# The seventh product's sum in the routing's PSUM banks, and a new order of steps, in the 512-token pages

## The chip, the cores and the metric

The kernel runs on one core of one Trainium2 chip. The metric is the device time of one execution in microseconds, the median of the runs shown. Matrix products run on TensorE (PE in the profile; its weight loads are PEld), elementwise work on VectorE (DVE) and ScalarE (ACT), indirect DMAs are issued by GpSimd (POOL) and all other DMAs by SyncE (SP). Each engine works through its own instructions in the order in which the kernel wrote them, and waits for the other engines where data or a buffer asks for it. TensorE writes its sums to PSUM, which has eight banks; one bank holds 128 x 512 float32 values.

## The reference

A gated scan over four sequences of 5056 tokens with 256 channels gives y, and y goes through a mixture of eight experts, of which each token uses one:

```python
a_t = np.exp(8.0 * sig_r * np.log(a_base))
x_gated = np.sqrt(np.maximum(1.0 - a_t * a_t, 1e-06)) * sig_i * x
for t in range(S):
    h = a_t[:, t] * h + x_gated[:, t]
    y[:, t] = h

logits = x @ w_gate + modality_bias[modality_id]
e_idx = np.argmax(logits, axis=1)
gate_w = probs[np.arange(N), e_idx]
for e in range(E):
    mask = e_idx == e
    h = np.maximum(x[mask] @ w1[e], 0.0)
    out[mask] = gate_w[mask, None] * (h @ w2[e])
```

There are N = 20224 tokens, D = 256 channels and FF = 1024 hidden units.

## The kernel before

**Stages.** The sequences are loaded in 23 chunks; each is scanned, split into two float16 parts (a high part and the rest), and routed: TensorE computes the logits, VectorE the places, and the tokens' rows are written to DRAM sorted by expert. Two experts get most tokens, and their weights stay on the chip. From the sorted rows the kernel builds pages of one expert's tokens: a few of 128, most of 256, and, once all chunks are loaded and sums of weight blocks are there, pages of 512 (`WIDE`). Experts with few tokens get 128-token pages with weights of their own, which ScalarE and VectorE convert (`cw`).

**The order.** A planner in the kernel writes every engine's instructions in order while the kernel is built. Each piece of work is a thread that names its engine, a length and a condition (`room` of a buffer tag, or a mark that something is `seen`); the planner takes what can start first. Times in it only decide the order; on the chip, waits are set by the data and the buffers.

**A page on TensorE.** `expert_layers` (from L1335) runs the first layer of a page in steps, and after each step some units of the second layer of the page before. A unit is three matmuls with 256 columns (two float16 parts of each operand, without the product of the two rests); a step of a 512-token page is six of them. `share` (L1285) says how many 32nds of the units follow each step; a 512-token page has 32 units, eight to each 128 tokens, a 256-token page has 16, a 128-token page 8.

**The 512-token pages.** Their first layer treats X·W1 as 2 x 2 blocks in Strassen's manner (Winograd's form): seven products instead of eight. `go(g, i)` issues product i for group g (half of the hidden units of each half), so a page has 14 steps, (0,1) to (1,4). A group has three PSUM sums of one bank each:

- `pa` (bank 1): product 1, then 2 on top. ScalarE copies product 1 into pb before that (`seed`, L1227).
- `pb` (bank 2): starts from that copy; 6, 5 and 3 are added. After 6 and after 5, ScalarE copies the sum out (v and v5, L1199).
- `pc` (bank 5): product 7; VectorE adds v5 (c22, L1204); then 4 on top, and VectorE adds v (c21).

Each of the four results goes through `relu_pair`: a relu on ScalarE (L1103) gives the high part, VectorE (L1105) the rest, into `Hx` and `Hg`, which the second layer reads. v, v5, c21 and c22 of a group lie in one buffer `sv` of tag `a` (three buffers, which the token sums `rf` also use). The sums of tokens T, which products 4 to 7 take, are made on VectorE and ScalarE from X while the page before runs.

**PSUM.** Tag `ph` has four banks, `po` (second layer) two, and `lg` two, which the routing uses (`psl`). In the 512-token pages pa, pb and pc all take banks of `ph` in turn, six to a page. A bank comes free when its last reader is done. A page's first use of a bank for pb needs a matmul before it that wrote the whole bank; where the bank last held a 128-token page, a matmul without use (L1247) writes it.

## Time and profile before

| | us |
|---|---|
| median of 3 runs | 978.96 |
| lowest, highest | 977.93, 980.19 |
| the profiled execution | 988.55 |
| its span, first to last instruction | 986.7 |
| TensorE busy in it | 878.6 |
| VectorE, ScalarE, GpSimd busy | 698.9, 671.0, 481.5 |

The profiled execution is one run with the hardware profiler; its durations and waits are those of that run. A row of a wait names who waited, for whom, the total, how often, and the longest. A row of the timeline gives a start, a duration, the engine, the line of the kernel, what was written from what, and in brackets how long the engine had been idle and what ended that. Matmul ends are modelled, so that groups of matmuls overlap a little on paper. A granted clock of 1.00 is TensorE's full speed.

### The profile page before, as it was taken

The page shows a single profiled execution, that of the slowest core. Times are in us where ns is not written, and L with a number is a line of the kernel's source. Part 1 is how long each engine was busy: PE and PEld are TensorE (multiplying, and loading weights), DVE is VectorE, ACT ScalarE, POOL GpSimd, SP SyncE. Part 2 cuts the span into 40 slices and gives each one's busy share as a digit, 9 for nine tenths or more (in the row PEclk, how much of TensorE's full clock was granted, in tenths as well). Part 3 has the DMA queues.
Part 4 walks back from the last instruction along what each step waited for, and adds up shares of the span by engine and source line. Part 5 has one row for each costly group of instructions (what it writes and reads, how often), then busy time and mean ns, then how long its engine had stood idle before and what let it go on. Part 6 is the DMA issues. An engine that isn't in the chain of part 4 may idle for free.

```text
span 986.7 us, 22224 instructions
## 1 busy us (share of the span) xinstructions
PE 878.6 (89%) x8461; PEld 775.3 (79%) x8461; DVE 698.9 (71%) x1535; ACT 671.0 (68%) x960; POOL 481.5 (49%) x506
## 2 busy tenths in 40 slices
PE   2358995989999998999999999998899999999896
PEld 1247884878888887888888888877788888888786
DVE  5976886697886787799678789686675656645451
ACT  6876886776887787897767989544655545444542
POOL 5233464577766676667575667363451111112121
PEclk9988997999999999999999999999999999999998
DMA  8757885878989798996889976965332222112410
GB/s 294 213 151 182 257 245 110 230 192 179 288 224 229 168 248 230 214 207 196 187 225 236 260 194 167 155 137 147 96 92 55 60 49 49 45 45 64 125 35 23
DMA packets 222759, 160.43 MB, mean 163 GB/s; under 512 B 197297, under 2 KB 201522, under 8 KB 216114
## 3 DMA queue, kind: packets, MB, share of 16 engines
q1 hardware_dynamic: 205714, 114.49, 51.0%
q0 software_dynamic: 16224, 44.25, 13.9%
q8 instruction: 68, 1.11, 0.5%
q14 instruction: 49, 0.40, 0.1%
q10 hardware_dynamic: 704, 0.18, 0.1%
HBM read 72.96 MB, written 44.48 MB: 119 GB/s over the span
## 4 chain that ended last, share of the span: by engine, by line
PE 53%; DVE 14%; issue 9%; DMA 9%; ACT 8%; POOL 3%; SPq 1%; another core or an unknown queue 0%; POOLq 0%; ACTq 0%; DVEq 0%
PE po L1326 26%; PE ph L1166 17%; PE pb L1256 4%; PE pc L1256 3%; DVE x L546 3%; DMA rows<-rt,di 3%; PE pa L1256 2%; DVE H L1105 2%; DMA rt<-a 2%; DMA X<-rows 2%; POOL out_dram L1121 2%; POOL rows L813 2%; DVE g L517 1%; ACT H L1103 1%; DVE x L531 1%
## 5 line engine op out<-in xcount | busy, mean ns | idle before, releaser
L1166 PE MATMUL ph<-X,hw 128*128 128x256 f16 (+1 forms) x2688 | 334.3, 276 | 23.7 <-DMA X<-rows 21.7
L1121 POOL DMA_INDIRECT out_dram<-ot,mt x160 | 206.6, 1291 | 282.5 <-ACT ot L1117 239.5
L1326 PE MATMUL po<-hw,H 128*128 128x256 f16 x2640 | 330.1, 274 | 11.4 <-issue 7.5
L1166 PEld LDWEIGHTS <-hw 128*128 128x128 f16 x2688 | 261.6, 100 | 57.9 <-DMA X<-rows 15.4
L813 POOL DMA_INDIRECT rows<-rt,di x158 | 214.9, 1360 | 183.6 <-PE ph L1166 44.7
L1326 PEld LDWEIGHTS <-H 128*128 128x128 f16 x2688 | 259.1, 98 | 46.9 <-issue 12.9
L1105 DVE SCALAR_TENSOR_TENSOR H<-ph,H 128x512 f16<-128x512 f32 (+1 forms) x232 | 151.6, 664 | 79.9 <-ACT H L1103 62.6
L1103 ACT ACTIVATE H<-ph 128x512 f16<-128x512 f32 (+1 forms) x232 | 132.9, 577 | 106.4 <-PE ph L1166 70.6
L1117 ACT ACTIVATE ot<-po,gt 128x256 f32<-128x256 f32 x160 | 75.3, 472 | 87.7 <-PE po L1326 75.8
L546 DVE TENSOR_TENSOR_SCAN x<-a,x 128x2048 f32<-128x2048 f32 (+2 forms) x23 | 87.9, 3821 | 0.8
L1326 PE MATMUL po<-hw,Hg 128*128 128x256 f16 x576 | 83.5, 273 | 0.0
L1326 PE MATMUL po<-hw,Hx 128*128 128x256 f16 x576 | 80.2, 273 | 0.6 <-ACT ot L1117 0.6
L1256 PEld LDWEIGHTS <-sw 128*128 128x128 f16 x576 | 56.5, 98 | 28.2 <-issue 21.5
L1326 PEld LDWEIGHTS <-Hx 128*128 128x128 f16 x576 | 56.2, 98 | 7.2 <-issue 0.7
L1326 PEld LDWEIGHTS <-Hg 128*128 128x128 f16 x576 | 56.4, 98 | 6.5
L663 ACT ACTIVATE a<-x,scy 128x1024 f16<-128x1024 f32 (+2 forms) x46 | 45.8, 1021 | 17.5 <-DVE scy L289 15.3
L531 DVE TENSOR_TENSOR x<-g,x 128x2048 f32<-128x2048 f32 (+2 forms) x23 | 45.8, 1989 | 16.4 <-ACT x L529 14.4
L1204 DVE TENSOR_TENSOR sv<-pc,sv 128x512 f32<-128x512 f32 x48 | 33.1, 690 | 29.6 <-PE pc L1256 16.2
L1199 ACT ACTIVATE sv<-pb 128x512 f32<-128x512 f32 x48 | 28.6, 595 | 34.2 <-PE pb L1256 34.1
L666 DVE SCALAR_TENSOR_TENSOR a<-x,scy,a 128x1024 f16<-128x1024 f32 (+2 forms) x46 | 50.8, 1121 | 1.2 <-ACT a L663 1.1
L522 ACT ACTIVATE a<-a,ch 128x1024 f32<-128x1024 f32 (+2 forms) x46 | 50.8, 1119 | 0.0
L1105 DVE SCALAR_TENSOR_TENSOR Hg<-sv,Hg 128x512 f16<-128x512 f32 x48 | 33.1, 690 | 24.2 <-ACT Hg L1103 20.7
(210 smaller groups left out, 1118.2 us busy)
## 6 DMA issues: line engine op xcount, KB each, us to landing
a<-in_r_gate_dram SPq DMA_DIRECT2D x17, 1024.0 KB
g<-in_i_gate_dram SPq DMA_DIRECT2D x17, 1024.0 KB
x<-in_x_dram SPq DMA_DIRECT2D x17, 1024.0 KB
wr<-in_moe_w_dram SPq DMA_DIRECT2D x4, 1024.0 KB
cr<-in_moe_w_dram SPq DMA_DIRECT2D x4, 1024.0 KB
a<-in_r_gate_dram SPq DMA_DIRECT2D x5, 512.0 KB
g<-in_i_gate_dram SPq DMA_DIRECT2D x5, 512.0 KB
x<-in_x_dram SPq DMA_DIRECT2D x5, 512.0 KB
```

The lines of the kernel that those rows point to most:

```text
L522: nc.scalar.activation(sl, sl, AF.Exp, scale=ch[:, h : h + 1], bias=ch[:, h : h + 1])
L531: nc.vector.tensor_tensor(out=y, in0=g, in1=y, op=ALU.mult)
L546: nc.vector.tensor_tensor_scan(out=y, data0=a, data1=y, initial=0.0, op0=ALU.mult, op1=ALU.add)
L666: nc.vector.scalar_tensor_tensor(out=ys[:, 1, :, u, :], in0=yg[:, :, u, :], scalar=sc, in1=ys[:, 0, :, u, :], op0=ALU.mult, op1=ALU.subtract,)
L813: ins = nc.gpsimd.indirect_dma_start(out=rows[:, :], out_offset=bass.IndirectOffsetOnAxis(ap=idx, axis=0), in_=src, in_offset=None, bounds ...
L1103: nc.scalar.activation(hi, src, AF.Relu)
L1105: nc.vector.scalar_tensor_tensor(out=lo, in0=src, scalar=0.0, in1=hi, op0=ALU.max, op1=ALU.subtract)
L1117: nc.scalar.activation(ot, po, AF.Copy, scale=t.gt[:, a : a + 1])
L1121: ins = nc.gpsimd.indirect_dma_start(out=out[:, :], out_offset=bass.IndirectOffsetOnAxis(ap=t.mt[:, a, 0:1], axis=0), in_=ot, in_offset=No ...
L1166: ins = nc.tensor.matmul(ph[:, v, 0:st], lhsT, rhs, start=(m == 0 and v == 0), stop=(m == len(mm) - 1), skip_group_check=True,)
L1256: ins = nc.tensor.matmul(to[:, v, :], lhsT[s], rhs[x], start=(i in (1, 7) and v == 0 and m == 0), stop=(m == 2), skip_group_check=True,)
L1326: ins = nc.tensor.matmul(prev.po, prev.h(hx, f, rs_), wv[:, wx, f], start=(prev.count == 1), stop=(prev.count == 3 * NF))
```

## The change

pc takes a bank of `lg` and not of `ph`, so that a 512-token page takes four banks of `ph` and both of `lg`. The bank of pc is given back after VectorE's second sum from it, as before. The 14 steps go in another order: group 1 starts third and not sixth, and step 4 of group 0 is thirteenth and not ninth. The numbers of second-layer units between the steps are spread anew; their sum stays 32.

```diff
             if then is not None:
                 yield from then
-            if bank_of is not None and src is not bank[g, bank_of][1]:
-                give("ph", bank[g, bank_of][0])
+            if bank_of == 5:
+                give("lg", bank[g, 5][0])
             fs = slice(2 * g, 2 * g + 2)
             ts = slice(256 * h, 256 * h + 256)
             yield from relu_pair(cur.H[fh][:, 0, fs, ts], cur.H[fh][:, 1, fs, ts], src, 1.0)
-            if bank_of is not None and src is bank[g, bank_of][1]:
+            if bank_of in (1, 2):
                 give("ph", bank[g, bank_of][0])
...
             if i == 7:
-                bank[g, 5] = take_bank(f"pc{cur.n}_{g}", True)
+                bank[g, 5] = take("lg"), psl.tile([P, 2, 256], F32, name=f"pc{cur.n}_{g}", tag="lg")
...
-        order_ = [(0, 1), (0, 7), (0, 6), (0, 2), (0, 5), (1, 1), (0, 3), (1, 7), (0, 4), (1, 6), (1, 2), (1, 5), (1, 3), (1, 4)]
-        share = [2, 2, 2, 2, 1, 2, 1, 2, 2, 3, 3, 5, 3, 2]
-        for (g, i), n in zip(order_, share):
+        steps_ = [(0, 1), (0, 7), (1, 1), (0, 6), (0, 2), (1, 6), (0, 5), (1, 7), (1, 5), (0, 3), (1, 2), (1, 3), (0, 4), (1, 4)]
+        share = [2, 2, 2, 2, 2, 3, 2, 3, 2, 2, 3, 3, 2, 2]
+        for (g, i), n in zip(steps_, share):
             conds = {
                 1: [room("ph", 2), room("a")] + ([ready, room("x"), room("g")] if g == 0 else []),
-                7: [room("ph"), seen(("T", cur.n))], 6: [seen(at(g, "seed"))], 2: [seen(at(g, "seed"))],
+                7: [room("lg"), seen(("T", cur.n))], 6: [seen(at(g, "seed"))], 2: [seen(at(g, "seed"))],
                 5: [seen(at(g, "v"))], 3: [seen(at(g, "v5"))], 4: [seen(at(g, "c22"))],
```

## The prediction

> **What bounds the kernel now.** I read the totals first, then TensorE's waits by stretch of the span, then the windows and the timeline of the stretch that the change touches.

> ```profile
> span 986.7 us, 22224 instructions
> PE 878.6 (89%) x8461; PEld 775.3 (79%) x8461; DVE 698.9 (71%) x1535; ACT 671.0 (68%) x960; POOL 481.5 (49%) x506
> L791 DVE TENSOR_TENSOR be<-be,psl x23: 142/155/156, 31.0 to 660.8; 128x8 f32<-128x8 f32 x23
> L1256 PE MATMUL pc<-T,sw x144: 269/272/418, 682.2 to 930.8; 128*128 128x256 f16 x144
> L1256 PE MATMUL pc<-T,hw x144: 272/273/418, 693.5 to 941.5; 128*128 128x256 f16 x144
> ```

> The reader is to see that TensorE is busy for nine tenths of the span, that the routing reads its PSUM for the last time at 660.8 us, and that the 512-token pages run from 681 to 942 us, after it. There are 12 of them: (144 + 144) matmuls into pc, 24 to a page. Nothing that the change edits runs before 681 us.

> TensorE's waits from 681 to 942.5 us ("who: total us, times, longest us"):

> ```profile
> PE pc L1256 <- DVE Hx L1105: 16.4, 11, 3.2
> PE pc L1256 <- DVE rf L1050: 1.5, 1, 1.5
> PE pb L1256 <- ACT sv L1199: 1.1, 3, 0.4
> PE ptc L301 <- ACT cw L297: 0.6, 1, 0.6
> PE po L1326 <- ACT ot L1117: 0.6, 1, 0.6
> ```

> One wait for each of the 12 pages, 17.9 of the 21.2 us, stands before a group into pc. Its place is in the timeline of one page (start, duration, engine, line; in brackets the idle time before it):

> ```profile
> 837.77 0.49 PE L1326 MATMUL po<-hw,Hg 128*128 128x256 f16 x3
> 838.72 0.68 DVE L1105 SCALAR_TENSOR_TENSOR Hx<-pb,Hx 128x512 f16<-128x512 f32 x1
> 839.45 0.81 PE L1256 MATMUL pc<-T,sw 128*128 128x256 f16 x6 [1.19 <-DVE Hx L1105]
> 840.11 0.82 PE L1326 MATMUL po<-hw,Hx 128*128 128x256 f16 x6
> ```

> pc of group 1 is the sixth bank that a page takes from the four of `ph`, so it gets the bank of group 0's pb. VectorE reads that bank last, in the relu after step (0,3), and ends at 839.40; TensorE starts at 839.45. So the bank is what holds it. The one wait put down to rf is the same place, with a VectorE instruction ahead of that relu.

> What a wait costs is read from the distance between starts, because a group's 0.82 us reaches 0.16 us past the start of the next:

> ```profile
> 657.59 1.47 PE L1166 MATMUL ph<-X,hw 128*128 128x256 f16 x12
> ...
> 679.86 1.47 PE L1326 MATMUL po<-hw,H 128*128 128x256 f16 x12
> ```

> Between these two starts seventeen groups of 12 matmuls pass without a wait: 22.27 / 204 = 0.1092 us each. Now the windows (stretch, its us, busy us of PE, PEld, DVE, ACT, POOL with counts, granted clock, DMA share, GB/s):

> ```profile
> 688.00:691.60 3.60, 0.42 (x5) 0.22 (x3) 3.53 (x8) 2.21 (x4) 1.48 (x2) 0.97 1.04 372
> 691.60:695.10 3.50, 3.50 (x18) 2.48 (x18) 0.12 (x1) 0.00 (x0) 0.87 (x1) 0.54 0.29 96
> 829.59:850.60 21.01, 19.82 (x183) 17.61 (x181) 12.20 (x21) 10.98 (x20) 3.89 (x4) 1.00 0.28 53
> 905.86:920.49 14.63, 12.11 (x110) 10.55 (x109) 9.11 (x15) 8.62 (x16) 0.97 (x1) 1.00 0.20 38
> 920.49:942.24 21.75, 20.10 (x184) 17.72 (x182) 11.20 (x20) 13.97 (x23) 3.89 (x4) 1.00 0.50 137
> 681.17:892.48 211.31, 195.30 (x1758) 172.44 (x1756) 129.80 (x255) 112.94 (x202) 57.31 (x56) 0.99 0.31 71
> ```

> A full page, 84 matmuls of its own and 96 of the page before, would take 180 x 0.1092 = 19.65 us. It takes 21.01: 1.36 lost, which is the 1.19 of its wait and the 0.16 (1.35). The first ten pages take 211.3 us where 132 + 9 x 180 matmuls need 191.3 (the first has half as much second layer beside it): 20.0 lost. The eleventh loses 14.63 - 108 x 0.1092 = 2.8, the twelfth 21.75 - 19.65 = 2.1. So 24.9 us are lost in all, and no change of order or banks can win more there.

> **The change, part by part.**

> *pc in the routing's banks.* The 12 waits go: 17.9 + 12 x 0.16 = **19.8 us**. Both `lg` banks are free from 660.8 on. Each page takes them once: (0,7) and (1,7).

> *What the first wait drags with it.* After its 3.2 us the granted clock of the next 3.5 us is 0.54 (windows above): 3.5 x 0.46 = **1.6 us**, which I count as gone with the wait. Pages with waits of 1.2 us keep a clock of 1.00. If the slow stretch came from the transfers ahead of it instead (DMA share 1.04), it would stay, and the sum be 1.6 less. [...]

> *The new order.* It decides whether other waits take the place. Durations in a page:

> ```profile
> 824.35 0.82 PE L1256 MATMUL pb<-T,sw 128*128 128x256 f16 x6
> 825.20 0.60 ACT L1199 ACTIVATE sv<-pb 128x512 f32<-128x512 f32 x1 [1.04 <-PE pb L1256]
> ...
> L1204 DVE TENSOR_TENSOR sv<-pc,sv 128x512 f32<-128x512 f32 x5 | 3.5, 691 | 2.9 <-ACT sv L1199 1.6 <-PE pc L1256 1.3
> L1105 DVE SCALAR_TENSOR_TENSOR Hg<-sv,Hg 128x512 f16<-128x512 f32 x4 | 2.8, 689 | 1.9 <-ACT Hg L1103 1.9
> L1103 ACT ACTIVATE Hg<-sv 128x512 f16<-128x512 f32 x4 | 2.5, 622 | 0.2 <-DVE sv L1204 0.2
> L1117 ACT ACTIVATE ot<-po,gt 128x256 f32<-128x256 f32 x4 | 1.9, 474 | 3.4 <-PE po L1326 3.3
> L1061 ACT ACTIVATE T<-rf 128x512 f16<-128x512 f32 x2 | 1.3, 630 | 1.5 <-DVE rf L1054 1.5
> L1227 ACT ACTIVATE pb<-pa 128x512 f32<-128x512 f32 x2 | 1.2, 585 | 0.4 <-PE pa L1256 0.4
> ```

> A step lasts 6 x 0.1092 = 0.655 us and a unit of the second layer half of that. With the new shares the steps of a full page start at: (0,1) 0; (0,7) 1.3; (1,1) 2.6; (0,6) 3.9; (0,2) 5.2; (1,6) 6.6; (0,5) 8.2; (1,7) 9.5; (1,5) 11.1; (0,3) 12.4; (1,2) 13.8; (1,3) 15.4; (0,4) 17.0; (1,4) 18.4; end 19.65. ScalarE can read a step's bank 0.85 us after its start (824.35 to 825.20) and needs 0.6 for a copy, so 1.45 from a step to the one that needs its copy. The seed is there at 1.45 for (0,6) at 3.9, and at 4.1 for (1,6) at 6.6; v at 5.4 for (0,5) at 8.2, and at 8.0 for (1,5) at 11.1; v5 at 9.7 for (0,3) at 12.4, and at 12.6 for (1,3) at 15.4. The spare time is 2.4 to 3.1 us. c22, 0.69 later than v5, is there over 5 us ahead of its step 4. Queued on ScalarE ahead of a copy can be an eviction (0.47), a relu (0.62) and a T copy (0.63), 1.7 together: covered.

> Banks: pb of group 1 is free at 15.4 + 0.85 + 0.6 + 0.7 = 17.6, and next wanted at 19.65 + 2.6. pc of group 0 is read by 18.6 and wanted at 20.95; pc of group 1 by 20.6 and wanted at 29.2. The second layer of the next page begins with H of (0,3), done by 15.3, and reaches (1,3)'s at its fifth unit, 23.0. Then SP's queue, and T:

> ```profile
> SPq L1091 <- PE pa L1256: 140.5, 11, 15.5
> 844.30 0.69 DVE L1063 TENSOR_TENSOR T<-rf,T 128x512 f16<-128x512 f32 x1 [0.32 <-ACT T L1061]
> ```

> The input transposes wait on SP for the last reads of their X buffers, (1,2) and (1,3), which now stand 5.9 and 4.3 us before the page's end. T of the page that starts at 850.6 was complete at 845.0, 6.9 us ahead of its step 7; a page 1.35 shorter leaves over 5.

> Two pages have less beside them. With 16 units (the first) the spare time is 1.5 us or more, with 8 (the eleventh, after the 128-token page) 1.1. There a queue on ScalarE may cost some tenths. The three waits for sv (1.1 + 3 x 0.16 = 1.6 us) stood in those two pages; whether they go, or others like them come, I leave at nothing, with 1.6 either way. The cold experts' conversions put the longest pieces on ScalarE, in three pages, as before:

> ```profile
> L297 ACT ACTIVATE cw<-cr 128x2048 bf16<-128x2048 f32 x3 | 5.7, 1906 | 0.0
> ```

> Each is shorter than a full page's spare time; with a relu behind it, it could cost some 0.6.

> *The dummy matmul.*

> ```profile
> L1247 PE MATMUL pb<-hw x1: 379/379/379, 905.6 to 905.6; 128*128 128x512 f16 x1
> ```

> It stands where a bank of pb held a 128-token page. With four banks in a fixed turn, both pb of the eleventh page need it: one more, of 512 columns, twice 0.109: **+0.2**. DMAs, SP's and POOL's queues get no instruction more or less; the last pages are TensorE's chain and move up as a whole.

> Sum: -19.8 - 1.6 + 0.2 = **-21.2 us**, bounds -22.8 (sv waits go and nothing comes) and -17.8 (the slow clock stays, and 3 x 0.6 in the cold pages come). The profiled execution took 988.55 us (1.85 around its span): 967.3. The same microseconds from the median, 978.96, give **957.8**. The median run is 1% shorter than the profiled one; where, the trace can't say, but a wait set by VectorE and TensorE durations should be the same in both.

> **The rivals.**

> 1. *The sum buffers hold the page start.* Group 1 now starts third and group 0's step 4 is thirteenth, so both sv live for the whole page, in a pool of three that also holds rf. sv of group 0 is read last by the relu after (0,4): 17.0 + 0.82 + 0.69 + 0.62 + 0.69 = 19.8, or 20.6 if group 1's sum goes first on VectorE. The planner holds the next (0,1) for that, up to 1.0 after 19.65. If the chip does too, 10 pages that follow a wide one lose 1.0: 957.8 + 10 = 968. Against it: the first instruction that writes the buffer is the copy v on ScalarE, at 19.65 + 4.8, and TensorE shows no wait on Hg's readers now. For it: nothing but the planner's condition.

> 2. *ScalarE becomes the bound (slower).* It runs its queue in order, and an instruction planned too early blocks those behind it. The place is a T copy that waits for rf:

> ```profile
> 735.75 0.63 ACT L1061 ACTIVATE T<-rf 128x512 f16<-128x512 f32 x1 [2.50 <-DVE rf L1054]
> ```

> Ahead of a copy v or v5 that would be 2.5 + 2 x 0.63 = 3.8 us against a spare 2.4: 1.4 + 0.16 on TensorE. At two of the six copies of every page it is 12 x 3.1 = 37, and 995. It turns the sign from 21.2 / 12 = 1.8 us a page on. Against it: this idle time ran beside TensorE's own wait, and ScalarE is busy for only 10.98 of a page's 21.01 us.

> 3. *Nothing changes:* the bank wait returns at another bank, 1.35 a page, 979. The margins above speak against it.

> 4. *A denser TensorE gets a lower clock.* From 657.59 to 679.86 it runs without a gap, and its stretch has

> ```profile
> 656.00:681.00 25.00, 25.00 (x234) 22.42 (x232) 14.06 (x43) 8.74 (x16) 10.96 (x13) 1.00 0.48 100
> ```

> a clock of 1.00. The wide pages need 261 - 13 (the 128-token page) - 21 = 227 us; a mean clock below 227 / 248 = 0.91 would eat the gain, and at 0.90 the time would be 958 + 25 = 983. [...]

> **How the numbers follow.** Forecast 0.76, by itself 955 to 962. Rival 1 0.13 (962 to 970), rival 2 0.05, rival 3 0.04, rival 4 0.02. The likeliest is 957.8. The range reaches from 954 (22.8 gained, and 2 for the spread of the medians) to 969, which takes in most of rival 1. Faster by over 0.2% (about what a measurement of this kernel can tell from no change) 0.89, within 0.2% 0.04, slower 0.07.

> **What would show it.** Right: no wait of TensorE into pc; pages 19.65 us apart from start to start; a clock of 1.00 after 690 us; two dummy matmuls; the last 45 us as long as now. Wrong: waits of pb on sv (rival 2), of pa on Hg (rival 1), or of pa, pb or pc on another reader (rival 3). The whole forecast fails if the page's period isn't set by TensorE once the bank is there.

## The result, and the profile after

| | before | after | after / before |
|---|---|---|---|
| time, median | 979.18 us (977.93 to 980.19, 4 runs) | 953.08 us (949.02 to 954.37, 4 runs) | 0.9727 [0.9695, 0.9759] |
| the profiled execution | 988.55 us | 952.39 us | |
| its span | 986.7 us | 950.5 us | |
| 512-token pages, from the first (0,1) to the next 256-token page | 681.17 to 942.24: 261.07 us | 668.81 to 905.84: 237.03 us | |
| from there to the end | 44.46 us | 44.66 us | |

The change makes the kernel 26.1 us faster. The forecast was 21.2 us faster, 957.8, in a range from 954 to 969: **the direction and the mechanism hold, the size is too small, and the time lies 0.9 us below the range.**

The two spans differ by 36 us, and 12 of these are no effect of the change: the pages start 12.36 us earlier (681.17 and 668.81), and nothing that is edited runs before them. The last section shows where most of them can come from. So in what follows each stage is measured by itself, from the start of a matmul group to the start of another.

The head of the profile's page and the three lines of matmuls that the prediction pointed at, of the kernel after (count, then shortest / median / longest ns, first and last start, shape):

```profile
span 950.5 us, 22224 instructions
PE 869.7 (91%) x8462; PEld 775.0 (82%) x8462; DVE 700.0 (74%) x1535; ACT 671.6 (71%) x960; POOL 484.7 (51%) x506
L1247 PE MATMUL pb<-hw x2: 379/379/379, 873.8 to 875.7; 128*128 128x512 f16 x2
L1256 PE MATMUL pc<-T,sw x144: 269/273/273, 669.8 to 896.1; 128*128 128x256 f16 x144
L1256 PE MATMUL pc<-T,hw x144: 272/273/273, 681.3 to 905.1; 128*128 128x256 f16 x144
```

There are two dummy matmuls in place of one, as many matmuls into pc as before, and the longest of them is now 273 ns where it was 418: no matmul into pc runs at a lower clock any more. Of TensorE's waits from 668 us, the start of the pages, to the end of the span, the trace of the kernel after lists none; before there were five rows, with 20.2 us. The windows say the same (stretch, its us, busy us of PE, PEld, DVE, ACT and POOL with counts, granted clock, DMA share, GB/s). They are pages 1, 2, 8, 11 and 12 from start to start:

```profile
668.81:683.36 14.55, 14.55 (x136) 13.06 (x134) 12.60 (x37) 11.58 (x20) 6.60 (x8) 1.00 0.93 245
683.36:703.47 20.11, 20.02 (x185) 17.73 (x183) 18.21 (x33) 14.61 (x25) 9.30 (x9) 1.00 0.42 99
821.37:841.02 19.65, 19.65 (x183) 17.61 (x181) 12.27 (x21) 10.85 (x20) 3.89 (x4) 1.00 0.18 43
874.04:886.05 12.01, 12.01 (x111) 10.66 (x109) 8.76 (x15) 8.72 (x16) 0.97 (x1) 1.00 0.20 46
886.05:905.84 19.79, 19.79 (x184) 17.75 (x182) 9.92 (x19) 13.23 (x23) 3.89 (x4) 1.00 0.53 152
```

The busy time of PE is the length of the stretch (but for 0.09 us in the second), at a clock of 1.00. A full page was 21.01 us with 19.82 busy and is 19.65; the first was 20.52 and is 14.55; the eleventh was 14.63 and is 12.01. Of the pages with 180 matmuls only the second, with a cold expert's weights to convert, is clearly longer, by 0.46 us: 0.14 for two small matmuls of the conversion (`ptc`), and some 0.3 in stops too short to be listed as waits. The twelfth holds such a pair too.

ScalarE now waits less for the groups into pb, whose sums it copies (stretch of the pages; the kernel before, then the kernel after):

```profile
ACT sv L1199 <- PE pb L1256: 34.1, 34, 2.8
```

```profile
ACT sv L1199 <- PE pb L1256: 24.3, 30, 1.1
```

It still waits, 30 times: ScalarE has time left in the pages and isn't their bound.

### The profile page after: what moved, and what is told of

Same layout as the page of the kernel before. It is cut to its first block, busy times and chain, and to the rows that moved or that the text cites. A ratio compares the mean times of both kernels' runs of the same rounds, so it can differ in the third digit from the quotient of the medians.

```text
span 950.5 us, 22224 instructions
## 1 busy us (share of the span) xinstructions
PE 869.7 (91%) x8462; PEld 775.0 (82%) x8462; DVE 700.0 (74%) x1535; ACT 671.6 (71%) x960; POOL 484.7 (51%) x506
## 4 chain that ended last, share of the span: by engine, by line
PE 46%; issue 21%; DVE 11%; DMA 8%; POOL 7%; ACT 6%; POOLq 0%; SPq 0%; ACTq 0%; DVEq 0%
PE po L1326 21%; PE ph L1166 21%; POOL out_dram L1121 5%; DMA rows<-rt,di 3%; DVE x L546 3%; DVE H L1105 2%; DMA X<-rows 2%; DMA rt<-a 2%; POOL rows L813 1%; PE pb L1256 1%; DVE x L531 1%; ACT H L1103 1%; PE psl L679 1%; PE pa L1256 1%; DVE g L517 1%
## 5 line engine op out<-in xcount | busy, mean ns | idle before, releaser
L1166 PE MATMUL ph<-X,hw 128*128 128x256 f16 (+1 forms) x2688 | 332.1, 276 | 27.3 <-DMA X<-rows 27.3
L1326 PE MATMUL po<-hw,H 128*128 128x256 f16 x2640 | 328.1, 274 | 2.9 <-DVE H L1105 2.7
L1121 POOL DMA_INDIRECT out_dram<-ot,mt x160 | 195.3, 1221 | 259.7 <-ACT ot L1117 217.9
L813 POOL DMA_INDIRECT rows<-rt,di x158 | 229.4, 1452 | 173.3 <-issue 40.7
L1166 PEld LDWEIGHTS <-hw 128*128 128x128 f16 x2688 | 261.3, 100 | 59.5 <-DMA X<-rows 21.3
L1326 PEld LDWEIGHTS <-H 128*128 128x128 f16 x2688 | 259.5, 98 | 35.0 <-DVE H L1105 3.5
L1105 DVE SCALAR_TENSOR_TENSOR H<-ph,H 128x512 f16<-128x512 f32 (+1 forms) x232 | 151.8, 665 | 80.0 <-ACT H L1103 79.6
L1103 ACT ACTIVATE H<-ph 128x512 f16<-128x512 f32 (+1 forms) x232 | 133.2, 578 | 99.9 <-PE ph L1166 88.1
L1117 ACT ACTIVATE ot<-po,gt 128x256 f32<-128x256 f32 x160 | 75.2, 471 | 50.5 <-PE po L1326 43.5
L1326 PE MATMUL po<-hw,Hx 128*128 128x256 f16 x576 | 81.8, 273 | 0.1
L1326 PE MATMUL po<-hw,Hg 128*128 128x256 f16 x576 | 80.2, 273 | 0.0
L1326 PEld LDWEIGHTS <-Hx 128*128 128x128 f16 x576 | 56.2, 98 | 6.7 <-issue 0.3
L1326 PEld LDWEIGHTS <-Hg 128*128 128x128 f16 x576 | 56.4, 98 | 6.5
L1256 PEld LDWEIGHTS <-sw 128*128 128x128 f16 x576 | 56.4, 98 | 6.5
L1103 ACT ACTIVATE Hg<-sv 128x512 f16<-128x512 f32 x48 | 30.0, 627 | 26.5 <-DVE sv L1204 26.2
L517 DVE SCALAR_TENSOR_TENSOR g<-g,x 128x2048 f32<-128x2048 f32 (+2 forms) x23 | 45.6, 1984 | 2.9 <-ACT g L513 2.9
L1199 ACT ACTIVATE sv<-pb 128x512 f32<-128x512 f32 x48 | 28.6, 595 | 25.9 <-PE pb L1256 24.3
```

The lines of the kernel that those rows point to most:

```text
L517: nc.vector.scalar_tensor_tensor(out=g, in0=g, scalar=1.0, in1=x, op0=ALU.add, op1=ALU.mult)
L813: ins = nc.gpsimd.indirect_dma_start(out=rows[:, :], out_offset=bass.IndirectOffsetOnAxis(ap=idx, axis=0), in_=src, in_offset=None, bounds ...
L1103: nc.scalar.activation(hi, src, AF.Relu)
L1105: nc.vector.scalar_tensor_tensor(out=lo, in0=src, scalar=0.0, in1=hi, op0=ALU.max, op1=ALU.subtract)
L1117: nc.scalar.activation(ot, po, AF.Copy, scale=t.gt[:, a : a + 1])
L1121: ins = nc.gpsimd.indirect_dma_start(out=out[:, :], out_offset=bass.IndirectOffsetOnAxis(ap=t.mt[:, a, 0:1], axis=0), in_=ot, in_offset=No ...
```

## The experiments

The theory: what the pages lose is TensorE's idle time, nearly all of it for a bank of PSUM, and the change removes it. Open were: whether the banks or the order do it; whether the spread of the second-layer units or a placement of the instructions that has nothing to do with either matters; what the first page's wait of 3.2 us, with the low clock after it, is worth; and why the gain is larger than forecast. The kernels ran on three chips, each with runs of the kernel before on the same chip; "pages" is the stretch from the first (0,1) to the next 256-token page, in each run's profile.

| run | chip | pages, us | ratio to the kernel before |
|---|---|---|---|
| e1 before again | A | 259.50 | 0.9985 [0.996, 1.001] |
| e2 after again | A | 237.02 | 0.9737 [0.971, 0.9764] |
| e3 banks only | A | 243.86 | 0.9768 [0.974, 0.9796] |
| e4 order and spread, four banks | A | 244.47 | 0.9812 [0.9782, 0.9841] |
| e5 before, one memset more | A | 263.58 | 1.0 [0.9971, 1.0028] |
| e6 after, other shares | A | 238.45 | 0.9773 [0.9737, 0.9809] |
| e7 after, units last | A | 242.85 | 0.9848 [0.98, 0.9896] |
| e8 banks only, units last | A | 266.76 | 1.0062 [1.0029, 1.0096] |
| e9 first page's bank only | B | 260.68 | 0.9969 [0.9948, 0.9991] |
| e10 banks only | B | 239.79 | 0.9771 [0.9731, 0.9811] |
| e11 order and spread, four banks | B | 241.04 | 0.98 [0.9756, 0.9843] |
| e12 after again | B | 237.02 | 0.9725 [0.9685, 0.9765] |
| e13 to e16 before again | C | 263.54, 260.43, 263.27, 260.27 | (one run each: 975.21 to 977.32 us; 975.17 beside them) |

### The two kernels again (e1, e2, e12, e13 to e16)

No edit: the kernel before in e1 and e13 to e16, the kernel after in e2 and e12.

> The kernel before once more, unchanged. The changed kernel gained 26.1 us by the medians, while its 512-token pages, from the first matmul of the first to the last of the twelfth, are 24.0 us shorter (237.0 against 261.1). Theory A: the 2 us over that are spread of the stage before those pages, which the change does not touch; then a ratio of 0.998 to 1.002 here, and in this profile pages that again last 261 us, with a first page that starts anywhere between 668 and 682 us. Theory B: the stage before is faster because of the change; then this profile has its first page at 680 us or later and the changed kernel's at 669 or earlier.

> The changed kernel once more, with more rounds. Theory A: its gain is that of the 512-token pages, 24.0 us, a ratio of 0.9755, interval within 0.972 to 0.978; pages of 237.0 us. Theory B: 26 us or more, a ratio of 0.973 or less, with a first page that starts earlier than in the profile of before beside it.

> The changed kernel beside the three above, on the same chip: pages of 237.0 us and no wait of TensorE in them, a gain of 24 us and what the stage before happens to differ by (2 us either way).

> The kernel before, one look. The changed kernel gains 26 us on three chips (26.7, 26.0, 26.2, each with 2 either way), its pages 24.4 against the mean of three profiles of before (261.1, 259.5, 263.6). Theory A (the pages of before vary with the clock after the idle times of the first two pages, and last longer on average than those three show): the four looks lie between 259 and 265 us, their mean at 262 or more. Theory B (the remaining 2 us are in the stage before the pages): mean 261 or less.

> The kernel before, a second look, for the same mean; and a second case of what the clock does after the idle times of the first and the second page: halved where the idle time is 3 us or more (theory A), or without regard to it (theory B).

> The kernel before, a third look, for the same mean and the same clock.

> The kernel before, a fourth look, for the same mean and the same clock.

The pages of the kernel after took 237.03, 237.02 and 237.02 us. Those of the kernel before (with e5, whose pages are the same) took 259.50 to 263.58 in seven profiles, 261.7 on average. Without idle time of TensorE the pages agree within 0.01 us, with waits they lie 4.08 us apart. So the pages give 261.7 - 237.0 = **24.7 us**, 24.0 against the one profile that the forecast was made from.

The spread of the kernel before is in its first two pages: from the third page on all seven took 217.97 to 217.99 us (before: 261.07 less 20.52 and 22.58). In e1 the bank is waited for 2.24 us in the first page, and the group after it takes 0.82 us, which is full speed:

```profile
698.71 0.82 PE L1256 MATMUL pc<-T,sw 128*128 128x256 f16 x6 [2.24 <-DVE Hx L1105]
```

In e13 it is 3.76 us, and the same six matmuls take 1.44 us; 1.7 us of waiting in the second page bring a slow group again:

```profile
675.76 1.44 PE L1256 MATMUL pc<-T,sw 128*128 128x256 f16 x6 [3.76 <-DVE Hx L1105]
...
698.06 1.21 PE L1256 MATMUL pc<-T,sw 128*128 128x256 f16 x6 [1.71 <-DVE Hx L1105]
```

The three comparisons of the kernel after give 26.7 [23.6, 29.9], 26.1 [23.5, 28.8] and 26.9 us [23.0, 30.8] (one less the ratio, by the median of the kernel before beside it). The 24.7 us of the pages lie inside each of the three. That they are about 2 us below all three is left open: the stage ahead of the pages and the last 45 us are not edited, and of the rows read there none goes with the kernel rather than with the chip. What was expected on this point did not hold as written. e1 has the ratio expected for unchanged code and pages of 259.50 us, but its first page starts at 688.34 us, outside 668 to 682; e2 gains the 26.1 us of theory B, with a first page 5.1 us earlier than e1's; e12's 26.9 us are above the 24 with 2 either way; and e13 to e16 average 261.9 us, between the bounds of their two theories. The clock was low behind the wait of the first page in all four of these, whose waits were 3.17 us or more.

### Banks alone (e3, e10)

Against the kernel after, the old order and shares:

```diff
-        steps_ = [(0, 1), (0, 7), (1, 1), (0, 6), (0, 2), (1, 6), (0, 5), (1, 7), (1, 5), (0, 3), (1, 2), (1, 3), (0, 4), (1, 4)]
-        share = [2, 2, 2, 2, 2, 3, 2, 3, 2, 2, 3, 3, 2, 2]
-        for (g, i), n in zip(steps_, share):
+        order_ = [(0, 1), (0, 7), (0, 6), (0, 2), (0, 5), (1, 1), (0, 3), (1, 7), (0, 4), (1, 6), (1, 2), (1, 5), (1, 3), (1, 4)]
+        share = [2, 2, 2, 2, 1, 2, 1, 2, 2, 3, 3, 5, 3, 2]
+        for (g, i), n in zip(order_, share):
```

> pc in the routing's banks, with the order and the shares of before. Theory A (the wait for the bank is nearly all of it, and the old order has 0.8 us or more to spare for every copy in a full page): no wait of TensorE into pc, full pages of 19.65 us, a gain of 19.8 + 1.6 = 21.4 us less 0.2, the waits for sv in the short pages stay: 958, a ratio of 0.978; the new order is worth 2 to 3 us by itself. Theory B (the order matters as much: without it the wait goes to the copies of v and v5 on ScalarE): full pages of 20.3 us or longer, 966 or more.

> pc in the routing's banks with the order of before, a second time. The first profile has a wait of 2.0 us in the first page for a seed that ScalarE itself started late for nothing that the profile names, and a slow clock behind it, together about 3.8 us. Theory A (that was chance, the order's own worth is the rest): without it pages of 240 us, 3 us more than the changed kernel's, all of it in the first two pages, the eleventh and the twelfth. Theory B (the order of before brings it): again 2 us there, pages of 244 us.

Theory A held in both: the ratios are 0.9768 and 0.9771 where 0.978 was expected, and the full pages are 19.65 us. In e10 TensorE doesn't stand still for 160 us (window of the full pages, then all of its waits in the 512-token pages):

```profile
700.00:860.00 160.00, 160.00 (x1473) 143.46 (x1471) 99.91 (x189) 86.83 (x161) 40.63 (x40) 1.00 0.28 61
```

```profile
PE po L1326 <- ACT ot L1117: 1.9, 2, 1.3
PE pb L1256 <- ACT sv L1199: 0.4, 1, 0.4
```

The pages take 239.79 us, 21.9 less than the kernel before. What stays, 2.8 us more than the kernel after, is in pages 2 and 3 (41.29 us where the kernel after has 39.76), 11 (12.52 and 12.01) and 12 (20.51 and 19.79): pages with a conversion of weights on ScalarE or with less second layer beside them.

e3, the same kernel on another chip, lost 4.1 us more, 3.7 of it in the first page, which took 18.20 where e10 took 14.54. There one instruction of ScalarE began 1.99 us after the last that it followed, and the trace names nothing that it waited for ("remote"); TensorE then stood for its seed, and its clock fell (two rows of the timeline, then windows of 2 us):

```profile
687.06 0.58 ACT L1227 ACTIVATE pb<-pa 128x512 f32<-128x512 f32 x1 [1.99 <-remote]
687.70 1.01 PE L1256 MATMUL pb<-T,sw 128*128 128x256 f16 x6 [1.96 <-ACT pb L1227]
```

```profile
687.70:689.70 2.00, 2.00 (x12) 1.53 (x12) 1.90 (x4) 0.60 (x1) 0.00 (x0) 0.62 0.80 166
689.70:691.70 2.00, 2.00 (x12) 1.43 (x11) 0.58 (x2) 0.60 (x1) 0.00 (x0) 0.53 1.00 405
691.70:693.70 2.00, 2.00 (x20) 1.80 (x19) 1.23 (x5) 1.52 (x3) 0.00 (x0) 1.00 1.08 368
```

e4 has such a hold too, e10 and e11 don't. So the pages of e3 and e4 understate what banks or order alone are worth, by some 4 us in the one profile of each.

### Order alone, with four banks (e4, e11)

Against the kernel before; pc stays in `ph`. The order of the changed kernel itself can't be had with four banks, since group 1 would ask for a bank ahead of the step that frees it, so this one only swaps (1,7) and (1,6), and takes another spread (the expectation counts three second-layer units between (0,3) and (1,7); the edit puts six there, where before there was one):

```diff
-        order_ = [(0, 1), (0, 7), (0, 6), (0, 2), (0, 5), (1, 1), (0, 3), (1, 7), (0, 4), (1, 6), (1, 2), (1, 5), (1, 3), (1, 4)]
-        share = [2, 2, 2, 2, 1, 2, 1, 2, 2, 3, 3, 5, 3, 2]
+        order_ = [(0, 1), (0, 7), (0, 6), (0, 2), (0, 5), (1, 1), (0, 3), (1, 6), (0, 4), (1, 7), (1, 2), (1, 5), (1, 3), (1, 4)]
+        share = [2, 2, 2, 2, 2, 2, 2, 2, 2, 2, 2, 4, 3, 3]
```

> pc stays in the four banks of ph, six takes to a page, and only the order is changed, to one that asks for a bank later: step 7 of group 1 comes three second-layer units and two steps after (0,3) instead of right behind it, and the sixth and eighth of group 1 change places. Theory A (what costs is when the bank's last reader is done, 2.15 us after the start of (0,3), not the number of banks): no wait in full pages, 0.2 to 0.7 us in the two short ones: a gain of 21 to 23 us, 956 to 958. Theory B (six sums need six banks): some wait for a bank stays in every page, 0.7 us or more, 966 or more.

> The four banks of ph with an order that asks for a bank later, a second time. Theory A: no wait in full pages again; without the late seed of the first page (2.1 us and the slow clock behind it) pages of 240 to 241 us, 3 to 4 more than the changed kernel's. Theory B: again 2 us there, pages of 244 us.

In e11, the full pages' window and the waits:

```profile
700.00:860.00 160.00, 160.00 (x1468) 143.40 (x1467) 101.25 (x190) 89.33 (x162) 40.10 (x41) 1.00 0.27 62
```

```profile
PE po L1326 <- ACT ot L1117: 1.6, 2, 1.1
PE pb L1256 <- ACT pb L1227: 0.9, 2, 0.6
PE pb L1256 <- ACT sv L1199: 0.7, 1, 0.7
```

No group waits for a bank, with **no bank more**: 241.04 us, 20.7 less than the kernel before. The bank that group 1's pc gets is the same; it is only asked for two steps and five units later, 3.9 us after (0,3) starts, and VectorE has read it 2.15 us after that start. The swap and the spread were not run apart. With the spread of before the swap alone would put 3 x 0.655 + 5 x 0.328 = 3.6 us there, an estimate that would be enough. What cost 20 us was not that there were four banks but that one was asked for ahead of its last reader. e4, with the hold of ScalarE, gains 18.7 us where 21 to 23 were expected, e11 19.5. Either cure alone gets over four fifths of the pages' gain. The changed kernel is 2.8 us shorter than e10 and 4.0 shorter than e11, in the pages with a conversion or with little cover.

### The spread of the units (e6, e7, e8)

e6 and e7 against the kernel after; e8 against banks only, with the same line as e7:

```diff
-        share = [2, 2, 2, 2, 2, 3, 2, 3, 2, 2, 3, 3, 2, 2]
+        share = [2, 2, 2, 2, 2, 2, 2, 3, 3, 3, 3, 2, 2, 2]
```

```diff
-        share = [2, 2, 2, 2, 2, 3, 2, 3, 2, 2, 3, 3, 2, 2]
+        share = [0] * 13 + [32]
```

> The changed kernel with the second-layer units spread in another way between the same 14 steps (their sum stays 32). Every copy still has over 1.4 us in a full page. Theory A (TensorE waits for nothing in these pages, so the spread doesn't matter): pages of 237.0 us, no wait, the time within 0.3% of the changed kernel's. Theory B (the spread was fitted and carries part of the gain): waits for sv come back, 0.3 us a page or more, 241 us or more.

> The changed kernel with all second-layer units behind the 14th step, none between. Theory A (the order by itself keeps a copy's step and the step that needs it three steps apart, 1.97 us against the 1.45 that a copy takes): waits of at most 0.5 us a page, pages of 237 to 243 us. Theory B (the units between the steps are the cover): 2 us a page or more, 261 us or more.

> pc in the routing's banks, the order of before, all second-layer units behind the 14th step. Theory A (in that order some copies have only two steps, 1.31 us, and others one): 0.15 at each of steps 6, 5 and 3 of group 0, 0.2 and 0.9 at 5 and 3 of group 1, 1.6 us a page, 19 us more than with the units between: pages of about 263 us, 20 or more above the new order's. Theory B (the order makes no difference once the bank is there): within 5 us of the new order with its units last.

e6: 238.45 us; seven full pages of 19.65, and 1.4 us more than the kernel after, 1.2 of it in page 2 beside the conversion, where two waits (0.8 and 0.4 us) came up that theory A did not expect. The time is 0.2% above e2's. So which of the even spreads is taken doesn't matter in a full page, but the 1.4 us are half of the 2.8 by which the new order is ahead of banks alone. With all units behind the fourteenth step the two orders part. The new one still all but fills TensorE in the full pages (e7, four of them), and loses 5.8 us in all, 3.4 of it in the first two pages (15.3 and 22.77 us; the latter is far more than the 0.5 us a page that was expected):

```profile
760.00:840.00 80.00, 79.91 (x730) 71.20 (x729) 50.03 (x102) 41.55 (x81) 15.87 (x16) 1.00 0.26 56
```

Two steps stand between a step and the one that needs its copy, and these cover most of ScalarE's time by themselves. In the old order only (0,2) stands between (0,6) and (0,5), which needs its copy, and (1,3) stands right behind (1,5), whose copy it needs. There, with the banks given, a full page takes 21.97 us, 2.3 more than without waits where 1.6 were expected, and the wait for the bank is replaced by one for the copy (e8, one page's length, then its two largest rows of waits in all pages):

```profile
776.31:798.28 21.97, 20.61 (x180) 17.57 (x180) 12.01 (x21) 10.87 (x21) 4.13 (x5) 1.00 0.21 49
```

```profile
PE pb L1256 <- ACT sv L1199: 11.8, 14, 1.3
PE pb L1256 <- ACT pb L1227: 2.0, 7, 0.4
```

e8 is the one kernel here that is slower than before, 1.0062 [1.0029, 1.0096], although no bank is waited for: in the old order the second layer between the steps is what hides ScalarE.

### A memset more (e5)

```diff
+    nc.vector.memset(s256, 0.0)
     more_pages(2, (N + E * (P - 1)) // P)
```

> The kernel before with one memset of a buffer that is no longer used, on VectorE behind the last work of the pages. Three changed kernels took 2 to 6 us less than their 512-token pages explain, in a stage in which their instructions are those of before. Theory A (that stage differs from build to build and from run to run, whatever is changed): this kernel too may stand 2 us or more off the kernel before, its pages at 259 to 261 us. Theory B (the stage is shorter because of what was changed in the pages): ratio 0.998 to 1.002, and the first page at the same time as in the kernel before.

1.0 [0.9971, 1.0028]: one instruction more ahead of the stage, and with it other places of all that follows, changes nothing in the time that these runs can tell. The first page starts at 684.40 us, 3.9 earlier than in e1 on the same chip, so its start moves by that much without any edit of the pages.

### The first page's bank alone (e9)

Against the kernel before: group 1's pc of the first 512-token page takes a bank of `lg`, and its conditions and its giving back go with it.

```diff
             if i == 7:
-                bank[g, 5] = take_bank(f"pc{cur.n}_{g}", True)
+                if g == 1 and cur.n == first_wide[0]:
+                    bank[g, 5] = take("lg"), psl.tile([P, 2, 256], F32, name=f"pc{cur.n}_{g}", tag="lg")
+                else:
+                    bank[g, 5] = take_bank(f"pc{cur.n}_{g}", True)
```

> The kernel before, with one bank moved: pc of group 1 of the first 512-token page alone takes a bank of lg. Theory A (the idle time of TensorE in that page, 2.2 to 3.4 us in three profiles, also halves its clock for up to 6 us after it): no wait into pc and a clock of 1.00 in that page, and the page shorter by the wait, 0.16 and the slow stretch, 4 to 6 us; the other eleven waits stay: pages of 255 to 257 us, ratio 0.994 to 0.996. Theory B (the clock falls because of the transfers beside it): the clock is below 0.9 for 3 us there all the same, 3.3 us gained at most.

A miss: 260.68 us. The first page does what was expected, 15.38 us; the second took 25.65 where it had been 22.6 to 24.3 (windows: page 1, page 2 up to its wait, the 5 us behind it; then the timeline):

```profile
669.68:685.06 15.38, 14.71 (x137) 13.06 (x135) 12.33 (x37) 10.87 (x19) 6.77 (x7) 1.00 0.87 231
685.06:697.90 12.84, 9.21 (x83) 7.84 (x82) 10.17 (x19) 10.12 (x17) 8.10 (x7) 1.00 0.32 89
697.90:702.90 5.00, 4.99 (x31) 3.76 (x31) 4.01 (x9) 1.26 (x2) 0.20 (x1) 0.66 0.07 26
```

```profile
695.65 0.38 PE L301 MATMUL ptc<-ssc,onesf 128*128 128x1 f32 x2 [1.04 <-ACT cw L297]
697.91 0.82 PE L1261 MATMUL pc<-T,sw 128*128 128x256 f16 x6 [1.88 <-DVE Hx L1105]
```

The low clock went with the idle time into the next page. It answers a question of the prediction: in page 1 the DMA share is 0.87 and the clock 1.00; behind the idle time of page 2 the share is 0.07 and the clock 0.66. In e1, too, TensorE waited beside a DMA share of 1.09 (698.00 to 700.00 us, 1.29 of them busy) and kept its clock of 1.00. So **in these runs the low clock went with TensorE's idle time, not with the transfers**; the last section has the rows. And a wait that is removed alone can move its cost: of 3.5 to 5.9 us won in the first page (18.92 to 21.32 before) 1.4 to 3.1 came back in the second. The eleventh took 16.3 us where the profile before has 14.63, for the same reason: behind its wait of 2.16 us the clock was at 0.50 from 900.51 to 903.93 us, which is 1.7 us lost.

None of the runs points to a version faster than the changed kernel: its 512-token pages have next to no idle time of TensorE left to win.

## Why the prediction was right and wrong

**Right.** *The bound.* TensorE's idle time was the loss of the pages, and the place was group 1's pc: with that wait gone by banks (e10) or by order (e11), a full page is 19.65 us, the number that 180 x 0.1092 gave. *The pages.* First and eleventh came out at 14.55 and 12.01 us, within 0.15 us of what the matmul counts in the prediction give (132 and 108, and one dummy of 0.2 us more in the eleventh). *The dummy matmul.* Two, as counted. *The clock.* 1.00 in all pages after. That the low stretch was the wait's and not the transfers' was the author's estimate; in e9, with that wait gone, the first page keeps 1.00. In six profiles of the unchanged first page 3.17 to 3.76 us of idle time are each followed by a group of 1.44 us where 0.82 is usual; the last section has a low clock behind 1.71, and full speed behind 2.24. *The last 45 us.* 44.46 and 44.66.

**The rivals.** *Sum buffers:* it did not come. In the kernel after, TensorE goes on to (0,1) while VectorE still reads sv:

```profile
841.02 0.82 PE L1256 MATMUL pa<-X,hw 128*128 128x256 f16 x6
841.17 0.68 DVE L1105 SCALAR_TENSOR_TENSOR Hg<-sv,Hg 128x512 f16<-128x512 f32 x1
```

*ScalarE as the bound:* it didn't come with this spread of units. e8 shows a cousin of it: where the cover is gone, TensorE waits for the copies themselves, at 0.96 us a page more than before (21.97 less 21.01). ScalarE is busy there for only 10.87 of the 21.97 us, so it is the delay of a copy and not a full ScalarE. *Nothing changes* and *a lower clock* did not come.

**Wrong: the sum, and the low end of the range that was made from it.** The step that failed is the costing of the small waits. "The three waits for sv (1.1 + 3 x 0.16 = 1.6 us) ... I leave at nothing", and the rows for ptc and po (0.6 each) entered no term, neither as kept nor as gone. In the changed kernel all five waits are gone. (The "21.2 us" of waits in the prediction is a slip: its five rows add up to 20.2. No term used it.) By the same rows:

| term | forecast, us | shown, us |
|---|---|---|
| 12 waits for the bank | -19.8 | gone (no row) |
| low clock behind the first | -1.6 | gone (clock 1.00) |
| three waits for sv | 0 | -1.6 |
| ptc for cw, po for ot: 1.2 + 2 x 0.16 | not counted | -1.5 |
| one dummy more | +0.2 | +0.2 |
| sum | -21.2 | -24.3 |
| the pages, by their starts | | -24.0 |

The prediction had the right figure at hand and did not use it: the losses by page add up to 24.9 us, and a page table of 14.4, 12.0 and 19.65 with a spare time of 1.1 us or more in each says that nearly all of it goes. The bound of -22.8 counted sv alone as the best case; the best case of its own table was 24.9 less 0.2, and with the 2 us that it allowed for the medians the range would have reached to 952.3.

What is left between 24.0 and the 26.1 us measured is in two parts. The profile that the forecast was made from was a good one for the kernel before, by 0.6 us (261.07 against 261.7 on average), since the low clock comes and goes. The other 1.4 us lie inside the interval of the comparison and stay open.

One doubt of the prediction has a likely answer: "The median run is 1% shorter than the profiled one; where, the trace can't say." The last section has rows for it in the stage ahead of the pages, though on which chips the first profiles ran is not on record; carrying the same microseconds over to the median fits them.

## What to carry to other kernels

If groups wait for a buffer in a steady turn, look at which step asks for it and at who reads it last: to ask two steps and five units later was worth 20.7 us here, two buffers more 21.9, and two buffers with the new order 24.7. Where every page has a known number of matmuls, forecast the stage from its full length without idle time and then say which waits stay; a sum of only the large waits leaves out the small ones that go with them. Compare a stage from group start to group start, since two spans can differ by far more than the change does.

## What the runs showed of the hardware

```profile
694.91:698.33 3.42, 1.06 (x9) 0.78 (x9) 2.81 (x5) 2.80 (x6) 1.80 (x2) 1.00 0.22 77
698.33:701.74 3.41, 3.41 (x18) 2.36 (x17) 1.50 (x7) 0.00 (x0) 0.91 (x1) 0.50 0.00 0
```

```profile
699.39:702.80 3.41, 1.86 (x18) 1.66 (x18) 3.33 (x10) 1.20 (x3) 0.62 (x2) 1.00 0.14 51
702.80:706.22 3.42, 3.42 (x34) 3.07 (x32) 3.12 (x5) 2.17 (x5) 2.58 (x2) 1.00 0.11 39
```

Ahead of the pages the same busy time does not part them: in the profile of the kernel before, 1.58 us in 39 matmuls are followed by a clock of 0.50, and 1.47 us in 14 by one of 1.00:

```profile
148.66:152.07 3.41, 1.58 (x39) 1.41 (x37) 2.79 (x4) 3.41 (x3) 2.80 (x3) 1.00 0.22 78
152.07:155.48 3.41, 0.00 (x0) 0.00 (x0) 1.26 (x8) 3.38 (x3) 2.80 (x5) 0.50 0.22 77
203.27:206.68 3.41, 1.47 (x14) 1.17 (x12) 3.41 (x4) 0.91 (x2) 2.82 (x3) 1.00 0.49 120
206.68:210.10 3.42, 2.90 (x28) 2.53 (x28) 3.20 (x20) 2.99 (x5) 0.97 (x1) 1.00 0.96 295
```

So 1.54 and 1.76 us are figures of these pages and no border that holds elsewhere. What sets the clock is not shown; no run varied the busy time by itself.

**On one chip TensorE issues later.** TensorE's waits that the trace puts to "issue" (for nothing that it shows) before the pages are 17 in the profile of the kernel before, in two rows

```profile
PE po L1326 <- issue: 7.5, 13, 1.2
PE ph L1166 <- issue: 1.9, 4, 0.8
```

9.3 us in all (the rows round up), about as much as that profiled execution (988.55) was above the median (979.18). In the eight profiles of chip A, of both kernels and those between, there are 18 to 24, together 8.9 to 12.7 us; in those of chips B and C, and in the first profile of the kernel after, not one. On chip A the kernel before took 994.31 us, on chip B 977.04. So in these runs it goes with the chip and not with the kernel, and it can account for 9.3 of the 12.4 us by which the pages start earlier in the profile after.

**A hold of ScalarE.** In e3 and e4 the first seed of the first 512-token page began 2 us late (1.99 and 2.09) with no releaser in the trace, in e10 and e11, the same kernels on another chip, not. Its cause is open.
